# A long convolution on one core: the order of products, sums and inverses in the middle phase

## The chip, the cores and the metric

The kernel runs on one core of a Trainium2 chip. The time is the device time of one execution in microseconds; before the change it is the median of three runs. The engines are named as in the profile: PE (matrix products, with its weight loads as PEld), DVE (vector), ACT (scalar), POOL (GpSimd) and SP (which here only starts DMAs). Each works through its own instructions in order and waits for others by semaphores.

## The reference, cut to what matters

```python
def _attn_ref(x, v, pos_emb, w1, w2):            # x, v: 4 x 12800 x 128
    h_mlp = np.maximum(pos_emb @ w1, 0.0) @ w2
    h_filt = h_mlp * np.exp(-0.01 * pos)[:, None]
    u = x * v
    Uf = np.fft.rfft(u, n=2 * S, axis=1)
    Hf = np.fft.rfft(h_filt, n=2 * S, axis=0)
    y = np.fft.irfft(Uf * Hf[None], n=2 * S, axis=1)[:, :S]
    return x * y

def _moe_ref(x, w_val, conv_w, w_out):           # x is the result above
    gate_pre = sum(conv_w[k] * xp[:, k:k + S] for k in range(5))
    return (sigmoid(gate_pre) * (x @ w_val)) @ w_out
```

A causal convolution over 12800 positions is done by Fourier transforms, for 4 batches and 128 channels, and followed by a gated projection. All of it is in float32.

## The kernel before, in words

The sequence is split in J = 2 halves, and each half of 6400 positions into N1 = 100 times N2 = 64. The transform is done in two steps, with three phases one after the other, each with its own buffers:

1. The first transform step over the signal (and the filter's own transform). It writes its result `a_u` to DRAM.
2. The **middle phase**, which alone is changed: for each of the 100 outer frequencies the second transform step, the product with the filter's spectrum, and the first step of the way back. It reads `a_u`, works on two frequencies at a time (a pair; NP = 50 pairs) and writes `c_y` to DRAM.
3. The last step of the inverse transform, then gate and projection.

In the middle phase one pair p is made of the following.

- `load_pair(p)`: SP starts the load of the pair's part of `a_u` (1 MB), and every fourth pair that of a table of weights. Loads run two pairs ahead (`AHEAD`), in six buffers named `ld`.
- `filter_pair(p)`: four short products on PE, and three ACT instructions that put the filter's spectrum into `h_sb`.
- `spectrum(..., j, c)`: one product z of signal half j, real or imaginary part c, into one PSUM buffer `z_ps`. There are four such products a pair, called z00, z01, z10 and z11 here (half, part). The four `z_ps` buffers are used in turn, and the filter takes one as well: five a pair from four buffers.
- `times(...)`: DVE multiplies a z (from PSUM) with the filter (SBUF). From half 0: `va` (z00) and `vb` (z01), each of four blocks of 512 columns; from half 1: `vc` (z10) and `vd` (z11), each of two blocks.
- The sums. Output half 0 needs va[0:2] + vb[0:2]. Output half 1 needs va[2:4] + vb[2:4] + vc + vd. That is four additions of 128 x 1024, three on POOL and one on DVE.
- `inverse(p, j, v)`: four products on PE into `c_ps` (two buffers), and an ACT copy into `c_sb`. When both halves of a pair are in `c_sb`, ACT starts two DMAs to `c_y`.

A matmul of z or of the filter reads all 128 rows and writes 64 columns of the array; one of the inverse reads 64 rows and writes 128 columns. Two such matmuls stand side by side on the array as a pair. Each product in float32 is two instructions per matmul in the profile, so a z shows as x4, a filter and an inverse as x8.

The order on each engine in this phase is the order in which the code is written (`tc.manual_schedule()`); nothing is moved by a scheduler. The loop runs over periods: in one period the products of pair p, the sums of pair p and the inverses of pair p - 1 are issued. Before the change PE's order in a period is z10 and z11 of p, inverse 0 of p - 1, filter and z00 of p + 1, inverse 1 of p - 1, z01 of p + 1. On DVE it is va, vb, the add of p - 1 (L432), vc, vd. On POOL: va[0:2] + vb[0:2] (L441), vc + vd (L442), va[2:4] + vb[2:4] (L443).

Phases 1 and 3 are not touched; in the changed file their line numbers are five smaller behind the change.

Of the kernel before, what the change touches and what calls it, by code (L numbers as in the profile page):

```python
# [118 lines left out]
def tile_longconv_gate(  # L119
# [205 lines left out]
    with tc.tile_pool(name="p2", bufs=1) as p2, tc.tile_pool(name="ps2", bufs=1, space=PSUM) as ps2:  # L325
# [10 lines left out]
        def filter_pair(p):  # L336

            h_ps = bank().rearrange("p (c e) -> p c e", c=2)
            for c in range(2):
                for h in range(2):  # L340
                    nc.tensor.matmul(
                        out=h_ps[half[h], c], lhsT=ag[:, 2 * p + h].rearrange("p j e -> p (j e)")[:, half[c]],
                        rhs=w2bd.rearrange("p j d -> p (j d)"), start=True, stop=True)
            h_sb = p2.tile([128, 2, J, 2, D], F32, name="h_sb2", bufs=3)
            src = h_ps.rearrange("p c (j d) -> p c j d", j=J)
            nc.scalar.copy(out=h_sb[:, 0].rearrange("p j c d -> p c j d"), in_=src)
            nc.scalar.activation(h_sb[:, 1, :, 0], src[:, 1], AF.Copy, scale=-1.0)
            nc.scalar.copy(out=h_sb[:, 1, :, 1], in_=src[:, 0])
            return h_sb

        def spectrum(a2, wk, j, c):
            z = bank()
            for h in range(2):
                nc.tensor.matmul(out=z[half[h]], lhsT=wk[:, h, half[c]], rhs=a2[:, h, j], start=True, stop=True)  # L354
            return z
# [21 lines left out]
        def inverse(p, j, vt):  # L377
            wk = loaded[p][1]
            c_ps = ps2.tile([128, 2, BD], F32, name="c_ps", bufs=2)
            for c in range(2):  # L380
                for h in range(2):
                    nc.tensor.matmul(  # L382
                        out=c_ps[:, h], lhsT=wk[half[h], 2 + c], rhs=vt[half[h], c].rearrange("p b d -> p (b d)"),
                        start=(c == 0), stop=(c == 1))
            if j == 0:
                c_sb = p2.tile([128, 2, J, B, D], F32, name="c_sb", bufs=2)
                outs[p] = c_sb
            c_sb = outs[p]
            nc.scalar.copy(out=c_sb[:, :, j].rearrange("p h b d -> p h (b d)"), in_=c_ps)  # L389
            if j == J - 1:  # L390
                for h in range(2):
                    nc.scalar.dma_start(
                        out=c_y[:, 2 * p + h].rearrange("j p b d -> p j (b d)"),
                        in_=c_sb[:, h].rearrange("p j b d -> p j (b d)"))

        weights, loaded, outs = [], {}, {}
        filt_p, z0, v_p = {}, {}, {}
        AHEAD = 2

        def start_pair(p):  # L400
            filt_p[p] = filter_pair(p).rearrange("p s j c d -> p s (j c) d")

        def first(p):
            z0[p, 0] = spectrum(*loaded[p], 0, 0)

        def second(p):
            z0[p, 1] = spectrum(*loaded[p], 0, 1)

        with tc.manual_schedule():
            for p in range(-1, NP + 1):
                now, nxt, old = 0 <= p < NP, p + 1 < NP, 0 <= p - 1
                for q in range(AHEAD + 1) if p < 0 else (p + AHEAD,):
                    if q < NP and q not in loaded:
                        loaded[q] = load_pair(q)
                if now:
                    h = filt_p.pop(p)
                    z10 = spectrum(*loaded[p], 1, 0)
                    z11 = spectrum(*loaded[p], 1, 1)  # L420
                    va = p2.tile([128, 2 * J, B, D], F32, name="va", bufs=3)
                    vb = p2.tile([128, 2 * J, B, D], F32, name="vb", bufs=2)
                    times(va, z0.pop((p, 0)), h[:, 0], 2 * J)
                    times(vb, z0.pop((p, 1)), h[:, 1], 2 * J)
                if old:
                    oa, oc = v_p.pop(p - 1)
                    inverse(p - 1, 0, oa)
                if nxt:
                    start_pair(p + 1)
                    first(p + 1)  # L430
                if old:
                    nc.vector.tensor_tensor(oc, oc, oa[:, 2:4], op=ALU.add)  # L432
                    inverse(p - 1, 1, oc)
                if nxt:
                    second(p + 1)
                if now:
                    vc = p2.tile([128, 2, B, D], F32, name="vc", bufs=3)
                    vd = p2.tile([128, 2, B, D], F32, name="vd", bufs=2)
                    times(vc, z10, h[:, 0, 0:2], 2)
                    times(vd, z11, h[:, 1, 0:2], 2)  # L440
                    nc.gpsimd.tensor_tensor(va[:, 0:2], va[:, 0:2], vb[:, 0:2], op=ALU.add)  # L441
                    nc.gpsimd.tensor_tensor(vc, vc, vd, op=ALU.add)  # L442
                    nc.gpsimd.tensor_tensor(va[:, 2:4], va[:, 2:4], vb[:, 2:4], op=ALU.add)  # L443
                    v_p[p] = va, vc

    ag_pool.__exit__(None, None, None)

# [234 lines left out]
```

## Time and profile before

| | |
|---|---|
| runs | 1241.81, 1249.56, 1248.66 us; median 1248.66 |
| profiled execution | 1245.33 us, span from first to last instruction 1243.6 us |
| mean granted TensorE clock | 0.955 |
| busy | PE 1091.5 us (88%), DVE 981.3 (79%), POOL 707.4 (57%), ACT 621.4 (50%) |
| middle phase | first POOL addition at 379.1 us, last copy of `c_sb` at 809.6 us |
| DMA | 332.96 MB, 268 GB/s on average |

A span's rows give start, duration, engine, line of the kernel, operation, the tiles written and read, and in brackets how long the engine was idle before it and what ended that. `x8` means that eight instructions were put together in a row. `DVE L432` is the DVE addition of the sums, `POOL L441` to `L443` are POOL's. The ends of matmuls are modelled, so PE is read by starts. Where several events are waited for, the row names the one that came last by the profile, and that name can be of another engine than the real cause.

### The profile page before, as it was taken

How to read it: one execution, taken by the hardware profiler on the slowest of the kernel's cores; microseconds unless marked ns; L12 is line 12 of the kernel's file. 1: busy time of each engine (PE TensorE's matmuls, PEld its weight loads, DVE VectorE, ACT ScalarE, POOL GpSimd, SP SyncE). 2: the span in 40 equal slices, each digit the busy share in tenths (PEclk: the TensorE clock that was granted, in tenths of full speed). 3: DMA queues.
4: the chain of work that ended last, by engine and by line, in shares of the span. 5: the costliest groups of instructions: out<-in, count | busy, mean ns of one | idle time of the engine just before them, and what ended most of it. 6: DMA issues, size and time to landing. Idle time of an engine off the chain costs nothing. (4 is left out here: it accounts for less than half of the span.)

```text
span 1243.6 us, 15440 instructions
## 1 busy us (share of the span) xinstructions
PE 1091.5 (88%) x5244; PEld 483.2 (39%) x5244; DVE 981.3 (79%) x1133; ACT 621.4 (50%) x1000; POOL 707.4 (57%) x282
## 2 busy tenths in 40 slices
PE   2578999768759999999999999878999999999886
PEld 1344666433323333333333333333444444444442
DVE  6576444567719999999999999706999899999897
ACT  1234755667642343343333333316667666766763
POOL 0000000000005899999999999806898888898890
PEclk9789999888878999999999999969999999999999
DMA  9999999999976777778778776388899999999932
GB/s 215 276 307 338 337 318 320 293 298 344 304 257 254 262 275 269 271 279 298 277 275 297 275 279 241 135 233 221 244 280 284 270 263 267 288 271 263 294 133 105
DMA packets 78151, 332.96 MB, mean 268 GB/s; under 512 B 8622, under 2 KB 9818, under 8 KB 57338
## 3 DMA queue, kind: packets, MB, share of 16 engines
q1 hardware_dynamic: 36928, 202.00, 55.0%
q10 hardware_dynamic: 41146, 129.98, 28.7%
q8 instruction: 43, 0.70, 0.2%
q14 instruction: 34, 0.28, 0.1%
HBM read 200.87 MB, written 131.07 MB: 267 GB/s over the span
## 5 line engine op out<-in xcount | busy, mean ns | idle before, releaser
L441 POOL TENSOR_TENSOR va<-va,vb 128x1024 f32<-128x1024 f32 x50 | 156.9, 3138 | 397.8 <-DVE vb L359 397.8
L542 POOL TENSOR_TENSOR ext<-yr,xr 128x400 f32<-128x400 f32 x120 | 301.1, 2511 | 55.7 <-DVE yr L540 35.8
L557 DVE SCALAR_TENSOR_TENSOR gt<-ext,cw,gt 128x1600 f32<-128x1600 f32 x128 | 241.3, 1885 | 1.1 <-ACT gt L554 1.1
L389 ACT COPY c_sb<-c_ps 128x1024 f32<-128x1024 f32 x100 | 101.3, 1013 | 274.1 <-PE c_ps L382 269.7
L354 PE MATMUL z_ps<-ld 128*64 128x512 f32 x800 | 196.7, 611 | 12.2 <-DMA ld<-a_u 12.2
L286 ACT COPY st<-fp 100x1024 f32<-100x1024 f32 x128 | 130.0, 1030 | 123.7 <-PE fp L285 46.0
L258 DVE TENSOR_TENSOR xv<-xv 114x1024 f32<-114x1024 f32 x64 | 78.4, 1224 | 116.7 <-DMA xv<-in_xv_dram 115.8
L515 PE MATMUL sd<-ld,inv 100*64 100x512 f32 x512 | 132.1, 622 | 9.8 <-DMA ld<-c_y 9.8
L576 PE MATMUL o_ps<-gd,wout 128*128 128x400 f32 x256 | 112.6, 522 | 26.3 <-ACT o_sb L584 12.0
L359 DVE TENSOR_TENSOR vb<-z_ps,h_sb 128x2048 f32<-128x2048 f32 x50 | 114.5, 2291 | 25.1 <-ACT c_sb L389 24.7
L359 DVE TENSOR_TENSOR va<-z_ps,h_sb 128x2048 f32<-128x2048 f32 x50 | 114.0, 2279 | 24.7 <-DMA ld<-a_u 24.7
L442 POOL TENSOR_TENSOR vc<-vc,vd 128x1024 f32<-128x1024 f32 x50 | 118.2, 2364 | 15.4 <-DVE vd L359 10.3
L443 POOL TENSOR_TENSOR va<-va,vb 128x1024 f32<-128x1024 f32 x50 | 118.5, 2370 | 0.0
L522 ACT COPY sd_sb<-sd 128x512 f32<-128x512 f32 x128 | 76.5, 598 | 75.3 <-PE sd L515 64.2
L382 PE MATMUL c_ps<-vc,ld 64*128 64x512 f32 x400 | 101.7, 627 | 9.2 <-DVE vc L432 8.8
L566 PE MATMUL v_ps<-ext,wval 128*128 128x400 f32 x256 | 107.6, 502 | 0.0
L354 PEld LDWEIGHTS z_ps<-ld 128*64 128x64 f32 x800 | 55.3, 139 | 118.6 <-issue 91.7
L382 PE MATMUL c_ps<-va,ld 64*128 64x512 f32 x400 | 99.4, 615 | 0.1
L285 PE MATMUL fp<-us,fsd 64*100 64x512 f32 (+1 forms) x256 | 76.9, 680 | 23.1 <-ACT st L286 21.7
L539 DVE TENSOR_TENSOR yr<-tp,dif 128x204 f32<-128x204 f32 x128 | 45.8, 358 | 61.7 <-ACT dif L531 61.6
L529 PEld LDWEIGHTS tp<-ident,sd_sb 128*128 128x128 f32 x512 | 59.8, 143 | 78.1 <-PE sd L515 49.5
L529 PE MATMUL tp<-ident,sd_sb 128*128 128x128 f32 x512 | 81.6, 285 | 3.6 <-DVE yr L540 3.6
(74 smaller groups left out, 1623.7 us busy)
## 6 DMA issues: line engine op xcount, KB each, us to landing
c_y<-c_sb ACTq DMA_DIRECT2D x100, 512.0 KB
ld<-a_u SPq DMA_DIRECT2D x49, 1024.0 KB
xv<-in_xv_dram SPq DMA_DIRECT2D x64, 768.0 KB
a_u<-st ACTq DMA_DIRECT2D x64, 768.0 KB
ld<-c_y SPq DMA_DIRECT2D x64, 768.0 KB
xr<-in_xt_dram SPq DMA_DIRECT2D x32, 800.0 KB
out_dram<-o_sb ACTq DMA_DIRECT2D x32, 800.0 KB
ld<-in_tab_w_dram SPq DMA_DIRECT2D x12, 1024.0 KB
```

What stands on the lines that cost most here:

```text
L286: nc.scalar.copy(out=st[:, c], in_=fp.rearrange("k j e -> k (j e)"))
L354: nc.tensor.matmul(out=z[half[h]], lhsT=wk[:, h, half[c]], rhs=a2[:, h, j], start=True, stop=True)
L359: nc.vector.tensor_tensor(out, z.rearrange("p (b d) -> p b d", d=D).unsqueeze(1).to_broadcast([128, n, B, D]), h_sb.unsqueeze(2).to_broadc ...
L382: nc.tensor.matmul(out=c_ps[:, h], lhsT=wk[half[h], 2 + c], rhs=vt[half[h], c].rearrange("p b d -> p (b d)"), start=(c == 0), stop=(c == 1))
L441: nc.gpsimd.tensor_tensor(va[:, 0:2], va[:, 0:2], vb[:, 0:2], op=ALU.add)
L442: nc.gpsimd.tensor_tensor(vc, vc, vd, op=ALU.add)
L443: nc.gpsimd.tensor_tensor(va[:, 2:4], va[:, 2:4], vb[:, 2:4], op=ALU.add)
L515: nc.tensor.matmul(out=sd[c * N2:(c + 1) * N2], lhsT=inv[:, c], rhs=ct[c][:, r * B * D:(r + 1) * B * D], start=True, stop=True)
L529: nc.tensor.transpose(out=tp[:, b], in_=t[:, b], identity=ident)
L542: nc.gpsimd.tensor_tensor(e[:, r0 + r], yr, xr, op=ALU.mult)
L557: nc.vector.scalar_tensor_tensor(gt, rows(t, k), cw[:, k:k + 1], gt, op0=ALU.mult, op1=ALU.add)
L576: nc.tensor.matmul(out=o_ps, lhsT=wout, rhs=gd, start=True, stop=True)
```

## The change

The work is the same, in another order. In a period PE now runs z00 and z01 of p, the filter of p + 1, z10 and z11 of p in one run, then inverse 1 and inverse 0 of p - 1 in one run. The sum for output half 1 is built up in another order: POOL adds vb[2:4] to va[2:4], then adds vc to that, then does va[0:2] + vb[0:2]; DVE adds the result of the second to vd, one period later, between its va and its vb. `vc` has two buffers in place of three, `vd` three in place of two. `c_sb` is begun by half 1 and sent off after half 0.

```diff
-            if j == 0:
+            if j == J - 1:
                 c_sb = p2.tile([128, 2, J, B, D], F32, name="c_sb", bufs=2)
                 outs[p] = c_sb
...
-            if j == J - 1:
+            if j == 0:
                 for h in range(2):
                     nc.scalar.dma_start(
...
+        def add(eng, out, a, b):
+            eng.tensor_tensor(out, a, b, op=ALU.add)
...
         with tc.manual_schedule():
-            for p in range(-1, NP + 1):
-                now, nxt, old = 0 <= p < NP, p + 1 < NP, 0 <= p - 1
-                for q in range(AHEAD + 1) if p < 0 else (p + AHEAD,):
-                    if q < NP and q not in loaded:
-                        loaded[q] = load_pair(q)
-                if now:
-                    h = filt_p.pop(p)
-                    z10 = spectrum(*loaded[p], 1, 0)
-                    z11 = spectrum(*loaded[p], 1, 1)
+            for q in range(AHEAD):
+                loaded[q] = load_pair(q)
+            h_next, old = filt_of(0), None
+            for p in range(NP + 1):
+                if p + AHEAD < NP:
+                    loaded[p + AHEAD] = load_pair(p + AHEAD)
+                if p < NP:
+                    h = h_next
+                    z = {}
+                    for c in range(2):
+                        z[0, c] = spectrum(*loaded[p], 0, c)
                     va = p2.tile([128, 2 * J, B, D], F32, name="va", bufs=3)
                     vb = p2.tile([128, 2 * J, B, D], F32, name="vb", bufs=2)
-                    times(va, z0.pop((p, 0)), h[:, 0], 2 * J)
-                    times(vb, z0.pop((p, 1)), h[:, 1], 2 * J)
-                if old:
-                    oa, oc = v_p.pop(p - 1)
-                    inverse(p - 1, 0, oa)
-                if nxt:
-                    start_pair(p + 1)
-                    first(p + 1)
-                if old:
-                    nc.vector.tensor_tensor(oc, oc, oa[:, 2:4], op=ALU.add)
-                    inverse(p - 1, 1, oc)
-                if nxt:
-                    second(p + 1)
-                if now:
-                    vc = p2.tile([128, 2, B, D], F32, name="vc", bufs=3)
-                    vd = p2.tile([128, 2, B, D], F32, name="vd", bufs=2)
-                    times(vc, z10, h[:, 0, 0:2], 2)
-                    times(vd, z11, h[:, 1, 0:2], 2)
-                    nc.gpsimd.tensor_tensor(va[:, 0:2], va[:, 0:2], vb[:, 0:2], op=ALU.add)
-                    nc.gpsimd.tensor_tensor(vc, vc, vd, op=ALU.add)
-                    nc.gpsimd.tensor_tensor(va[:, 2:4], va[:, 2:4], vb[:, 2:4], op=ALU.add)
-                    v_p[p] = va, vc
+                    times(va, z[0, 0], h[:, 0], 2 * J)
+                if old is not None:
+                    add(nc.vector, old[1], old[1], old[0][:, 2:4])
+                if p < NP:
+                    times(vb, z[0, 1], h[:, 1], 2 * J)
+                    if p + 1 < NP:
+                        h_next = filt_of(p + 1)
+                    for c in range(2):
+                        z[1, c] = spectrum(*loaded[p], 1, c)
+                    vc = p2.tile([128, 2, B, D], F32, name="vc", bufs=2)
+                    vd = p2.tile([128, 2, B, D], F32, name="vd", bufs=3)
+                    times(vc, z[1, 0], h[:, 0, 0:2], 2)
+                    times(vd, z[1, 1], h[:, 1, 0:2], 2)
+                if old is not None:
+                    inverse(p - 1, 1, old[1])
+                    inverse(p - 1, 0, old[0])
+                if p < NP:
+                    add(nc.gpsimd, va[:, 2:4], va[:, 2:4], vb[:, 2:4])
+                    add(nc.gpsimd, va[:, 2:4], va[:, 2:4], vc)
+                    add(nc.gpsimd, va[:, 0:2], va[:, 0:2], vb[:, 0:2])
+                    old = va, vd
```

On POOL this is what stands in the queue for one pair in the middle of the phase, with what each instruction waits for; the numbers behind the names tell the buffers' generations apart. First before, from one pair's L441 to the next pair's:

```order
L441 TENSOR_TENSOR va_2594<-va_2594,vb_2595 128x1024 [waits DVE_49,Pool_49]
L442 TENSOR_TENSOR vc_2629<-vc_2629,vd_2630 128x1024 [waits DVE_49]
L443 TENSOR_TENSOR va_2594<-va_2594,vb_2595 128x1024
L441 TENSOR_TENSOR va_2644<-va_2644,vb_2645 128x1024 [waits DVE_49,Pool_49]
L442 TENSOR_TENSOR vc_2679<-vc_2679,vd_2680 128x1024 [waits DVE_49]
```

After the change all three come from the helper `add` (L403); the first is va[2:4] + vb[2:4], the second va[2:4] + vc, the third va[0:2] + vb[0:2]:

```order
L403 TENSOR_TENSOR va_2588<-va_2588,vb_2589 128x1024 [waits DVE_49]
L403 TENSOR_TENSOR va_2588<-va_2588,vc_2608 128x1024 [waits DVE_49,Pool_49]
L403 TENSOR_TENSOR va_2588<-va_2588,vb_2589 128x1024
L403 TENSOR_TENSOR va_2638<-va_2638,vb_2639 128x1024 [waits DVE_49]
L403 TENSOR_TENSOR va_2638<-va_2638,vc_2658 128x1024 [waits DVE_49,Pool_49]
```

The second addition waits for POOL's own first one, and the third waits for nothing of its own. On DVE, at about the same place, before:

```order
L359 TENSOR_TENSOR va_2594<-z_ps_2564,h_sb2_2560 128x2048 [waits DVE_49,PE_49,Activation_49]
L359 TENSOR_TENSOR vb_2595<-z_ps_2576,h_sb2_2560 128x2048 [waits PE_49,Activation_49]
L432 TENSOR_TENSOR vc_2579<-vc_2579,va_2544 128x1024 [waits DVE_49,Pool_49]
L359 TENSOR_TENSOR vc_2629<-z_ps_2588,h_sb2_2560 128x1024 [waits PE_49]
L359 TENSOR_TENSOR vd_2630<-z_ps_2591,h_sb2_2560 128x1024 [waits PE_49]
```

And after:

```order
L359 TENSOR_TENSOR va_2588<-z_ps_2582,h_sb2_2548 128x2048 [waits PE_49,Activation_49]
L403 TENSOR_TENSOR vd_2559<-vd_2559,va_2538 128x1024 [waits DVE_49,Pool_49]
L359 TENSOR_TENSOR vb_2589<-z_ps_2585,h_sb2_2548 128x2048 [waits PE_49,Activation_49]
L359 TENSOR_TENSOR vc_2608<-z_ps_2602,h_sb2_2548 128x1024 [waits PE_49]
L359 TENSOR_TENSOR vd_2609<-z_ps_2605,h_sb2_2548 128x1024 [waits PE_49]
```

The addition has moved from behind vb to between va and vb, and what it reads from POOL (va of the pair before) is now written by POOL's second addition of that pair instead of its third. On PE, before, from an inverse 0 to the next inverse 1 (a product that is several instructions of the profile is one or two rows here):

```order
L382 MATMUL c_ps_2548<-va_2494,ld_2378 128x512 [waits Pool_49]
L382 MATMUL c_ps_2548<-va_2494,ld_2378 128x512 x3
L341 MATMUL z_ps_2555<-w2bd_70,ag_90 64x256 [waits DVE_49]
L341 MATMUL z_ps_2555<-w2bd_70,ag_90 64x256 x3
L354 MATMUL z_ps_2564<-ld_2486,ld_2484 64x512 [waits DMAHW5_49,DMAHW4_49,DVE_49]
L354 MATMUL z_ps_2564<-ld_2486,ld_2484 64x512
L382 MATMUL c_ps_2568<-vc_2529,ld_2378 128x512 [waits DVE_49,Activation_49]
L382 MATMUL c_ps_2568<-vc_2529,ld_2378 128x512 x3
```

And after, from the filter, the third of the five products of a run, to the end of the inverses:

```order
L341 MATMUL z_ps_2543<-w2bd_70,ag_90 64x256 [waits DVE_49]
L341 MATMUL z_ps_2543<-w2bd_70,ag_90 64x256 x3
L354 MATMUL z_ps_2552<-ld_2428,ld_2378 64x512 [waits DVE_49]
L354 MATMUL z_ps_2552<-ld_2428,ld_2378 64x512
L354 MATMUL z_ps_2555<-ld_2428,ld_2378 64x512 [waits DVE_49]
L354 MATMUL z_ps_2555<-ld_2428,ld_2378 64x512
L382 MATMUL c_ps_2562<-vd_2509,ld_2378 128x512 [waits DVE_49,Activation_49]
L382 MATMUL c_ps_2562<-vd_2509,ld_2378 128x512 x3
L382 MATMUL c_ps_2569<-va_2488,ld_2378 128x512 [waits Activation_49,Pool_49]
L382 MATMUL c_ps_2569<-va_2488,ld_2378 128x512 x3
```

The two inverses (c_ps) now stand one behind the other, and z11 (z_ps_2555) waits for DVE to have read the buffer that it takes over.

More of the change, by code (lines that the diff above doesn't have):

```diff
@@ L396, in tile_longconv_gate, with filt_of @@
         weights, loaded, outs = [], {}, {}
-        filt_p, z0, v_p = {}, {}, {}
         AHEAD = 2
[L400 to L407, printed above, removed]
-        with tc.manual_schedule():
-            for p in range(-1, NP + 1):
-                now, nxt, old = 0 <= p < NP, p + 1 < NP, 0 <= p - 1
-                for q in range(AHEAD + 1) if p < 0 else (p + AHEAD,):
-                    if q < NP and q not in loaded:
-                        loaded[q] = load_pair(q)
-                if now:
-                    h = filt_p.pop(p)
-                    z10 = spectrum(*loaded[p], 1, 0)
-                    z11 = spectrum(*loaded[p], 1, 1)
+        def filt_of(p):
+            return filter_pair(p).rearrange("p s j c d -> p s (j c) d")
```

## The prediction

> **What bounds the kernel now.** I read the table of stages first, for the middle phase, which alone is changed.
>
> ```profile
> core 0: us, PE busy (x) PEld busy (x) DVE busy (x) ACT busy (x) POOL busy (x), PEclk, DMA share, GB/s
> 386.00:397.00 11.00, 8.25 (x30) 2.42 (x28) 10.54 (x6) 2.13 (x4) 7.57 (x5) 0.84 0.40 153
> ...
> 407.50:418.00 10.50, 8.57 (x32) 2.69 (x30) 10.05 (x6) 2.41 (x5) 6.76 (x4) 0.84 0.50 185
> ...
> 450.00:500.00 50.00, 50.00 (x240) 17.38 (x238) 46.72 (x31) 18.98 (x30) 46.89 (x19) 1.00 0.82 291
> ```
>
> From 450 to 500 us PE is never idle at full clock; DVE and POOL are at 94%. Everything is close to its limit, so what an instruction waits for matters more than its length. Near 390 and 410 us it is otherwise: DVE is full and PE idle for 2 to 3 us in 11. Next the timeline, one period of the steady part (start, duration, engine):
>
> ```profile
> 560.16 1.99 PE L382 MATMUL c_ps<-va,ld 64*128 64x512 f32 x8
> 560.84 1.22 DVE L432 TENSOR_TENSOR vc<-vc,va 128x1024 f32<-128x1024 f32 x1
> 561.06 3.22 POOL L441 TENSOR_TENSOR va<-va,vb 128x1024 f32<-128x1024 f32 x1 [0.40 <-DVE vb L359]
> 561.97 1.22 DVE L359 TENSOR_TENSOR vc<-z_ps,h_sb 128x1024 f32<-128x1024 f32 x1
> 562.08 1.08 PE L341 MATMUL z_ps<-w2bd,ag 128*64 128x256 f32 x8
> 562.99 1.03 PE L354 MATMUL z_ps<-ld 128*64 128x512 f32 x4
> 563.95 1.99 PE L382 MATMUL c_ps<-vc,ld 64*128 64x512 f32 x8
> 564.23 2.28 DVE L359 TENSOR_TENSOR va<-z_ps,h_sb 128x2048 f32<-128x2048 f32 x1
> 565.87 2.79 PE L354 MATMUL z_ps<-ld 128*64 128x512 f32 x12
> 566.35 0.14 PEld L354 LDWEIGHTS z_ps<-ld 128*64 128x64 f32 x2 [0.28 <-issue]
> 566.72 2.37 POOL L443 TENSOR_TENSOR va<-va,vb 128x1024 f32<-128x1024 f32 x1
> 567.06 2.29 DVE L359 TENSOR_TENSOR vb<-z_ps,h_sb 128x2048 f32<-128x2048 f32 x1 [0.55 <-ACT c_sb L389]
> 567.63 0.14 PEld L354 LDWEIGHTS z_ps<-ld 128*64 128x64 f32 x2 [0.29 <-issue]
> 568.59 1.99 PE L382 MATMUL c_ps<-va,ld 64*128 64x512 f32 x8
> ```
>
> The period is 568.59 - 560.16 = 8.43 us, and PE fills it. Look at the two engines at 560.84: the DVE add starts first, POOL's add 0.22 later, and POOL's takes 3.22 where the other POOL add here takes 2.37. Both read two SBUF operands. Which of them starts first is the whole question, and the first periods of the phase show the other case:
>
> ```profile
> 379.10 2.37 POOL L441 TENSOR_TENSOR va<-va,vb 128x1024 f32<-128x1024 f32 x1 [378.66 <-DVE vb L359]
> ...
> 383.76 2.36 POOL L443 TENSOR_TENSOR va<-va,vb 128x1024 f32<-128x1024 f32 x1
> ...
> 386.08 2.34 POOL L441 TENSOR_TENSOR va<-va,vb 128x1024 f32<-128x1024 f32 x1
> 386.15 3.35 DVE L432 TENSOR_TENSOR vc<-vc,va 128x1024 f32<-128x1024 f32 x1 [0.48 <-POOL va L443]
> ...
> 389.43 1.21 DVE L359 TENSOR_TENSOR vc<-z_ps,h_sb 128x1024 f32<-128x1024 f32 x1
> 389.56 2.41 PE L382 MATMUL c_ps<-vc,ld 64*128 64x512 f32 x8 [2.75 <-DVE vc L432]
> ...
> 391.90 4.02 PE L354 MATMUL z_ps<-ld 128*64 128x512 f32 x12
> ...
> 396.48 2.35 POOL L441 TENSOR_TENSOR va<-va,vb 128x1024 f32<-128x1024 f32 x1
> 396.56 3.36 DVE L432 TENSOR_TENSOR vc<-vc,va 128x1024 f32<-128x1024 f32 x1 [0.30 <-POOL va L443]
> ...
> 406.91 2.36 POOL L441 TENSOR_TENSOR va<-va,vb 128x1024 f32<-128x1024 f32 x1
> 406.99 3.37 DVE L432 TENSOR_TENSOR vc<-vc,va 128x1024 f32<-128x1024 f32 x1 [0.40 <-POOL va L443]
> ...
> 410.50 2.87 PE L382 MATMUL c_ps<-vc,ld 64*128 64x512 f32 x8 [1.93 <-DVE vc L432]
> 411.41 1.21 DVE L359 TENSOR_TENSOR vd<-z_ps,h_sb 128x1024 f32<-128x1024 f32 x1
> ...
> 412.70 2.36 POOL L442 TENSOR_TENSOR vc<-vc,vd 128x1024 f32<-128x1024 f32 x1 [3.43 <-DVE vd L359]
> ...
> 415.26 2.29 DVE L359 TENSOR_TENSOR vb<-z_ps,h_sb 128x2048 f32<-128x2048 f32 x1 [0.45 <-PE z_ps L354]
> ...
> 417.47 1.22 DVE L432 TENSOR_TENSOR vc<-vc,va 128x1024 f32<-128x1024 f32 x1
> 417.70 3.23 POOL L441 TENSOR_TENSOR va<-va,vb 128x1024 f32<-128x1024 f32 x1 [0.32 <-DVE vb L359]
> ```
>
> Three times the DVE add waited for L443's result. It then started 0.07 to 0.08 us after POOL's next add, and took 3.35 to 3.37 us, not 1.22: it ended 1.07 to 1.09 us after POOL did. The add that comes second is held until the first is through. Those periods are 10.41 and 10.43 us long. At 417.47 a late vb delayed POOL's add, DVE came first, and POOL's add paid 0.86 us out of its own slack instead. From then on the period was 8.43.
>
> [...]
>
> **The change, part by part.**
>
> *PE.* The weight loads from 566.35 to 567.63 are three steps of a pair of matmuls each, 1.28 us, so 0.43 a pair. Three products are six pairs, 2.58 us, and their run takes 568.59 - 565.87 = 2.72: 0.14 for entering and leaving it. An inverse is four pairs, 1.72, and takes 562.08 - 560.16 = 1.92: 0.20. Each period has two runs of each kind, after the change one. PE's work falls by 0.34 to 8.09 us a period. That is worth 17 us only if PE stays the bound.
>
> *POOL and DVE.* Still three POOL adds and one DVE add, of the same shapes; no instruction goes. But the DVE add now reads va[2:4] after both vb and vc were added to it, and POOL's remaining add (va[0:2]) stands right behind that one, with no wait of its own. This is L443, L441 and L432 of the first periods again: DVE waits for a POOL result, and POOL's next add is always on its way before DVE hears of it. In the steady part of before the competing add, L441, needs vb, which stands directly ahead of the DVE add on DVE: DVE goes on at once, POOL hears of it later (417.47 against 417.70), and L443 is through by then (566.72 + 2.37 = 569.09, vb's end 569.35). After the change the competing add needs a vb that was done two POOL adds earlier, and the result that DVE waits for is the one just ahead of it. So I take the held length in every period.
>
> The loop that closes then: held add, times into vb, first POOL add, second POOL add, and the held add again. Step by step:
> - held add to the next DVE start: 389.43 - 386.15 = 3.28
> - vb: 2.29
> - from DVE's end to a POOL add that waits for it alone: 412.70 - (411.41 + 1.21) = 0.08
> - va[2:4] += vb: 2.36
> - POOL waiting for its own result, which before does not show. Low end 0.03: POOL's end to DVE's start, 386.15 - (383.76 + 2.36). High end 0.15: 417.70 - (415.26 + 2.29), DVE to a POOL add with two waits. I take 0.08, a single wait's row; the ends move the sum by -2.5 and +3.4 us over 49 periods
> - va[2:4] += vc until va[0:2] += vb starts: 386.08 - 383.76 = 2.32
> - from there to the DVE add: 0.08
>
> The sum is **10.49 us a period**, against 8.43.
>
> *What lies beside it.* PE has to bring inverse 1, inverse 0 and the next z between two held adds, and then va must be written: 0.14 (add's end at 406.99 + 3.37 to PE's start at 410.50), two inverses 3.84, z to its product on DVE 1.19 (565.87 to 567.06), va up to the following start 2.21 (2.28 less the 0.07 by which DVE starts its next instruction early, 389.43 against 386.15 + 3.35), an add without a hold 1.22: 8.60 of 10.49. So 1.89 us are spare, and the saved 0.34 lies in PE's idle time, worth nothing. If that cover went, the loop would be longer by what exceeds 1.89. Two waits are new. z11 takes z00's buffer of the four and so waits for DVE's va; behind it on PE stand the inverses, which need the add, and that is later anyway. POOL's second add waits for the first; behind it on POOL stands va[0:2], for which inverse 0 waits and which holds DVE, and both are in the loop above. ACT copies both c_sb halves one after the other, 2 x 1.01 in a period where it is busy 38%. The c_y DMAs go out once a period as before, and SP's loads wait for PE reads that are further apart; at 0.82 DMA share with 8.43 us there is more room at 10.49. vc's two buffers are written again two periods on, vd's three after three; POOL and inverse 1 have read them within one and two, so that delays nothing. Phases 1 and 3 keep their order.
>
> *The sum.* The end of before, first all 50 DVE adds (durations in ns, least, median, most; first and last start), then the last copy:
>
> ```profile
> L432 DVE TENSOR_TENSOR vc<-vc,va x50: 1215/1216/3368, 386.2 to 805.2; 128x1024 f32<-128x1024 f32 x50
> ```
>
> ```profile
> 809.60 1.01 ACT L389 COPY c_sb<-c_ps 128x1024 f32<-128x1024 f32 x1 [6.10 <-PE c_ps L382]
> ```
>
> The last of 50 adds starts at 805.2, the last c_sb copy at 809.60, 3.2 us behind the add's end. After the change POOL's first add starts at 379.10 as now, since vb of pair 0 is made as before. Its third add ends 2.36 + 0.08 + 2.32 + 2.35 = 7.11 later; 49 periods are 514.0; so POOL's last add ends at 900.2, the held add at 901.3, and the last copy comes 3.2 + 1.8 behind, since two inverses stand at the end: 906.3. That is 96.7 us later. Of this 46 x 2.06 = 95 is the hold; the three periods that were held already gain nothing. The profiled execution took 1245.33 us (span 1243.6), so 1342.0. The median of the runs, 1248.66, lies 3.3 above it; between 1342 and 1345.3 I say **1343**.
>
> **The rivals.**
>
> *The add is not held.* If DVE's add gets in ahead of POOL's third, DVE goes on after 1.13 (560.84 to 561.97), and the loop is 1.13 + 2.29 + 0.08 + 2.36 + 0.08 + 2.37 + 0.03 = 8.34, a little under today's 8.43. With the first three periods no longer held (3 x 2.1) and 46 x 0.09 that is 10 us less: 1236 to 1239, no slower, within 1%. It decides if DVE hears of the second add before POOL starts the third, so at the 0.07 us by which POOL led. Against it: three of three such meetings went to POOL. 0.05.
>
> *PE stays the bound and the merged runs pay.* Then 8.09 a period and the three periods free: 24 us less, 1222. It needs the two dependent POOL adds and vb inside 8.09, 0.25 less than the unheld loop has by its rows. 0.02.
>
> *The clock.* PE will idle about 2.4 us in 10.5. In the two stretches of the first view the granted clock is 0.84, and the run at 391.90 takes 4.02 instead of 2.79, that at 389.56 2.41 instead of 1.99: 1.65 together, still inside the 1.89. Two such slow spells in one period would cost 3.3, 1.4 over the spare time; in every third of 49 periods that is 23 us: 1366. 0.07.
> [...]
>
> **How the numbers follow.** Held add, PE within its spare time: 0.86, at 1343, from 1339 to 1348 by the bounds of POOL's own wait and the 3.3 us between profile and median. The range goes up to the clock's rival, and a few us down for what I have rounded: 1333 to 1366, which leaves out the two cases without a hold, 0.07, and worse clocks. A change of under 1% can't be told from none in this kernel. Slower by over 1%: 0.93 (held 0.86, clock 0.07); within 1%: 0.05; faster: 0.02.
>
> **What would show it.** In the changed profile the DVE add should take 3.3 to 3.4 us in nearly all of its 49 ordinary cases, start about 0.08 us after POOL's third add has started, and name POOL as what it waited for; POOL's third add should take 2.36, none 3.2. The period should be 10.4 to 10.6, with PE idle over 2 us in it ahead of the inverse and its runs without the two extra switches. I am wrong if DVE adds take 1.22 while POOL's take 3.2 (the order is not what I read from three rows), if the period is past 10.8 (PE's clock, or a longer wait of POOL on itself), or if phases 1 and 3 move by more than the spread of 1241.81 to 1249.56.

## The result, and the profile after

| | before | after |
|---|---|---|
| median of the runs made side by side | 1244.18 us (6 runs, 1241.26 to 1249.56) | 1346.26 us (6 runs, 1342.49 to 1354.44) |
| profiled execution, span | 1245.33 us, 1243.6 us | 1346.61 us, 1344.8 us |
| mean granted TensorE clock | 0.955 | 0.935 |
| last `c_sb` copy of the middle phase | 809.60 us | 905.92 us |

The ratio is 1.0804, with a 95% interval of 1.0767 to 1.0841: the change makes the kernel slower by 8%. Of the 101.2 us by which the span grew, 96.3 lie ahead of the last copy of the middle phase.

The table of stages for the middle phase after the change (length, busy time and number of instructions of each engine, granted clock, DMA share, GB/s):

```profile
core 0: us, PE busy (x) PEld busy (x) DVE busy (x) ACT busy (x) POOL busy (x), PEclk, DMA share, GB/s
...
450.00:500.00 50.00, 41.08 (x200) 16.04 (x200) 47.43 (x25) 15.81 (x25) 34.01 (x15) 1.00 0.63 225
550.00:600.00 50.00, 43.88 (x200) 17.18 (x196) 43.72 (x25) 15.62 (x25) 32.87 (x15) 0.93 0.68 236
```

Compare the first row with that of before: PE fell from 50.00 to 41.08 of 50 us, POOL from 46.89 to 34.01, and the DMA share from 0.82 to 0.63. DVE alone is as full as it was (47.43 against 46.72), though it ran 25 instructions and not 31. An engine that is as busy with fewer instructions has longer ones. All instructions of the helper `add`, grouped (durations in ns, least, median, most; first and last start), show which:

```profile
L403 POOL TENSOR_TENSOR va<-va,vb x100: 2330/2360/2383, 378.6 to 897.2; 128x1024 f32<-128x1024 f32 x100
...
L403 POOL TENSOR_TENSOR va<-va,vc x50: 2338/2370/2379, 381.0 to 894.9; 128x1024 f32<-128x1024 f32 x50
L403 DVE TENSOR_TENSOR vd<-vd,va x50: 1215/3297/3347, 383.4 to 897.3; 128x1024 f32<-128x1024 f32 x50
```

The median DVE add went from 1216 to 3297 ns. POOL's additions are all between 2330 and 2383: none of them takes 3.2 us any more. The timeline of one steady period:

```profile
598.92 2.37 POOL L403 TENSOR_TENSOR va<-va,vb 128x1024 f32<-128x1024 f32 x1 [3.36 <-DVE vb L359]
...
601.37 2.37 POOL L403 TENSOR_TENSOR va<-va,vc 128x1024 f32<-128x1024 f32 x1
...
601.62 2.29 DVE L359 TENSOR_TENSOR va<-z_ps,h_sb 128x2048 f32<-128x2048 f32 x1 [0.52 <-ACT c_sb L389]
...
603.71 2.34 POOL L403 TENSOR_TENSOR va<-va,vb 128x1024 f32<-128x1024 f32 x1
...
603.83 3.30 DVE L403 TENSOR_TENSOR vd<-vd,va 128x1024 f32<-128x1024 f32 x1
...
607.05 2.28 DVE L359 TENSOR_TENSOR vb<-z_ps,h_sb 128x2048 f32<-128x2048 f32 x1
...
607.28 1.99 PE L382 MATMUL c_ps<-vd,ld 64*128 64x512 f32 x8 [2.23 <-DVE vd L403]
...
609.41 2.38 POOL L403 TENSOR_TENSOR va<-va,vb 128x1024 f32<-128x1024 f32 x1 [3.37 <-DVE vb L359]
...
610.91 1.94 PE L354 MATMUL z_ps<-ld 128*64 128x512 f32 x8
...
614.32 3.31 DVE L403 TENSOR_TENSOR vd<-vd,va 128x1024 f32<-128x1024 f32 x1
```

POOL's third addition starts at 603.71, the DVE add 0.12 us behind it, and the add ends at 607.13, 1.08 us after POOL. Then vb follows, POOL waits 3.37 us for vb, and its next chain of three begins. The add itself shows no wait: POOL's second addition is through at 603.74, and DVE's own va, at 603.91, is through last. The period is 614.32 - 603.83 = 10.49 us. PE idles 2.23 us ahead of the inverse in it, and the two inverses, one behind the other, take 610.91 - 607.28 = 3.63.

### The profile page after: what moved, and what is told of

Same layout as the page of the kernel before. It is cut to its first block, busy times and chain, and to the rows that moved or that the text cites. A ratio compares the mean times of both kernels' runs of the same rounds, so it can differ in the third digit from the quotient of the medians.

```text
span 1344.8 us, 15454 instructions
## 1 busy us (share of the span) xinstructions
PE 1105.9 (82%) x5244; PEld 505.5 (38%) x5244; DVE 1053.7 (78%) x1133; ACT 622.7 (46%) x1000; POOL 668.2 (50%) x282
## 5 line engine op out<-in xcount | busy, mean ns | idle before, releaser
L403 POOL TENSOR_TENSOR va<-va,vb 128x1024 f32<-128x1024 f32 x100 | 235.9, 2359 | 543.1 <-DVE vb L359 543.1
L389 ACT COPY c_sb<-c_ps 128x1024 f32<-128x1024 f32 x100 | 101.2, 1012 | 289.0 <-PE c_ps L382 289.0
L382 PE MATMUL c_ps<-vd,ld 64*128 64x512 f32 x400 | 119.3, 718 | 92.8 <-DVE vd L403 92.7
L403 DVE TENSOR_TENSOR vd<-vd,va 128x1024 f32<-128x1024 f32 x50 | 139.4, 2788 | 3.1 <-POOL va L403 3.1
L403 POOL TENSOR_TENSOR va<-va,vc 128x1024 f32<-128x1024 f32 x50 | 118.3, 2366 | 3.9
L382 PEld LDWEIGHTS c_ps<-vd,ld 64*128 64x128 f32 x400 | 43.5, 209 | 160.9 <-issue 155.3
L382 PE MATMUL c_ps<-va,ld 64*128 64x512 f32 x400 | 103.8, 632 | 0.0
L354 PEld LDWEIGHTS z_ps<-ld 128*64 128x64 f32 x800 | 49.7, 136 | 126.0 <-issue 48.4
```

The lines of the kernel that those rows point to most:

```text
L382: nc.tensor.matmul(out=c_ps[:, h], lhsT=wk[half[h], 2 + c], rhs=vt[half[h], c].rearrange("p b d -> p (b d)"), start=(c == 0), stop=(c == 1))
L403: eng.tensor_tensor(out, a, b, op=ALU.add)
```

## The experiments

The theory: the new order makes the DVE add start behind POOL's third addition in every period; both read two operands from SBUF, the add is held until POOL's addition is through (3.30 us, where most adds of before take 1.22), and this closes a loop of 10.49 us. One rival says that the longer chain of dependent additions is what costs; another that DVE and POOL merely slow each other whenever they meet. Periods below are from the starts of like instructions in the profiled execution; those read from two rows lie within 0.02 us of the mean over the steady part.

### One operand of the add from PSUM

```diff
-                    add(nc.vector, old[1], old[1], old[0][:, 2:4])
+                    if p < NP:
+                        zb = z[0, 1].rearrange("p (b d) -> p b d", d=D).unsqueeze(1).to_broadcast([128, 2, B, D])
+                        nc.vector.tensor_tensor(old[1], zb, old[0][:, 2:4], op=ALU.add)
+                    else:
+                        add(nc.vector, old[1], old[1], old[0][:, 2:4])
```

> The changed kernel, with one operand of the DVE add taken from PSUM (the product z01 of the running pair) in place of vd, so that it reads one SBUF operand; its wait for POOL's second addition, its place and its length stay. (The summand vd is left out of the result.) Theory of the hold (a DVE instruction with two SBUF operands that starts after a POOL addition waits until that is through): the add takes 1.22 us beside POOL's third addition, the period falls from 10.49 to the longer of the loop through POOL, 8.34, and that through PE, 8.41; the time is 1346 - 49 x 2.05, about 1246. Rival, the chain (two dependent POOL additions and a wait set the period, and the long add only fills the waiting time): 10.49 stays, 1346. Rival, sharing (both engines slow down while they overlap, whoever starts): the add is somewhere between, about 2.2, the period about 9.5, 1297.

Measured: 1247.4 us (10 runs), 0.999 of before (0.9954 to 1.0025). In the timeline of this kernel:

```profile
598.42 2.36 POOL L403 TENSOR_TENSOR va<-va,vb 128x1024 f32<-128x1024 f32 x1
598.49 1.23 DVE L423 TENSOR_TENSOR vd<-z_ps,va 128x1024 f32<-128x1024 f32 x1
...
599.86 1.99 PE L382 MATMUL c_ps<-vd,ld 64*128 64x512 f32 x8 [0.16 <-DVE vd L423]
...
606.91 1.23 DVE L423 TENSOR_TENSOR vd<-z_ps,va 128x1024 f32<-128x1024 f32 x1
```

The meeting is the same, 0.07 us behind POOL's third addition, but the add takes 1.23 us and the period is 8.42. The order of POOL's chain and the wait for its result are unchanged, so the chain alone doesn't cost the 2 us, and with one of its operands in PSUM the add isn't held here at all. What bounds now is the loop that the prediction put beside the held one: add 1.23, start of PE 0.14, two inverses 3.63, z to DVE 1.19, va 2.21, together 8.40. The inverses wait 0.16 for the add in each period, so even without the hold the merged runs of PE bring nothing in this order.

### POOL's third addition halved

```diff
-                    add(nc.gpsimd, va[:, 0:2], va[:, 0:2], vb[:, 0:2])
+                    add(nc.gpsimd, va[:, 0:1], va[:, 0:1], vb[:, 0:1])
```

> The changed kernel with POOL's third addition half as wide (512 columns in place of 1024; block 1 of va stays without its summand). Theory of the hold: that addition takes about 1.19 us, the DVE add ends 1.08 us after it and so takes about 2.15, the period falls by 1.17 to 9.32, the time by 57 to about 1289. Rival, the chain: the third addition is not in it, so 10.49 and 1346 stay. Rival, PE's clock: 10.49 stays.

Measured: 1295.07 us (4 runs), 1.0412 of before (1.0328 to 1.0496). Its timeline:

```profile
601.92 1.28 POOL L403 TENSOR_TENSOR va<-va,vb 128x512 f32<-128x512 f32 x1
602.05 2.23 DVE L403 TENSOR_TENSOR vd<-vd,va 128x1024 f32<-128x1024 f32 x1
...
611.47 2.23 DVE L403 TENSOR_TENSOR vd<-vd,va 128x1024 f32<-128x1024 f32 x1
```

With a POOL addition shorter by 1.08 us the DVE add is shorter by 1.07 (2.23 against 3.30) and ends 1.08 us after POOL again. The period is 9.41: what POOL's addition is shorter by, the loop is shorter by too. The expectation was off only in the length of the halved addition, 1.19 for 1.28.

### POOL's third addition put first

```diff
+                    add(nc.gpsimd, va[:, 0:2], va[:, 0:2], vb[:, 0:2])
                     add(nc.gpsimd, va[:, 2:4], va[:, 2:4], vb[:, 2:4])
                     add(nc.gpsimd, va[:, 2:4], va[:, 2:4], vc)
-                    add(nc.gpsimd, va[:, 0:2], va[:, 0:2], vb[:, 0:2])
```

> The changed kernel with POOL's additions in another order: va[0:2] + vb[0:2] first, then the two that the DVE add needs, so that POOL has nothing under way when that add starts. Theory of the hold: every DVE add takes 1.22, but the moved addition now stands in the loop itself: 1.13 + 2.29 + 0.08 + 2.33 + 2.36 + 0.08 + 2.37 + 0.03 = 10.67 a period, about 1355, no gain. Had the long add been the only cost, with no loop behind it, the period would fall to about 8.4 and the time to 1246.

Measured: 1358.39 us (4 runs), 1.0911 of before (1.0827 to 1.0996). Its timeline:

```profile
603.71 2.35 POOL L403 TENSOR_TENSOR va<-va,vc 128x1024 f32<-128x1024 f32 x1
606.10 1.23 DVE L403 TENSOR_TENSOR vd<-vd,va 128x1024 f32<-128x1024 f32 x1 [2.19 <-POOL va L403]
...
616.75 1.23 DVE L403 TENSOR_TENSOR vd<-vd,va 128x1024 f32<-128x1024 f32 x1 [2.16 <-POOL va L403]
```

Nothing holds the add, it takes 1.23, and nothing is gained, since three POOL additions now stand between vb and the add where there were two. The period is 10.67 (10.65 between these two rows). An add that waits and one that is held cost the loop nearly the same, about the length of the third addition. A short DVE add is therefore no proof of a good order.

### The order of before with the add one place later

```diff
+                if now:
+                    vc = p2.tile([128, 2, B, D], F32, name="vc", bufs=3)
+                    vd = p2.tile([128, 2, B, D], F32, name="vd", bufs=2)
+                    times(vc, z10, h[:, 0, 0:2], 2)
                 if old:
                     nc.vector.tensor_tensor(oc, oc, oa[:, 2:4], op=ALU.add)
                     inverse(p - 1, 1, oc)
...
                 if now:
-                    vc = p2.tile([128, 2, B, D], F32, name="vc", bufs=3)
-                    vd = p2.tile([128, 2, B, D], F32, name="vd", bufs=2)
-                    times(vc, z10, h[:, 0, 0:2], 2)
```

> The kernel before with one thing moved: its DVE add (and the inverse behind it) stands behind the times that makes vc, not ahead of it, so that POOL's first addition has started about 0.9 us before it. No dependence is added. Theory of the hold: the add is held until POOL's is through and takes about 2.5 us, POOL's additions all take 2.36, and the loop of POOL's addition, the held add, vd and the two other POOL additions is 2.36 + 1.08 + 1.13 + 0.08 + 2.33 + 2.33 = 9.3 a period; with 46 periods of 0.87 more, 1244 + 40 = 1284. Rival, sharing: the order of start does not matter, POOL's first addition still takes 3.2 and the DVE add 1.22, the period stays 8.43, 1244.

Measured: 1285.63 us (4 runs), 1.0318 of before (1.0233 to 1.0403). Its timeline, without anything of the change but the lost start:

```profile
603.42 2.37 POOL L442 TENSOR_TENSOR va<-va,vb 128x1024 f32<-128x1024 f32 x1
604.16 2.71 DVE L436 TENSOR_TENSOR vc<-vc,va 128x1024 f32<-128x1024 f32 x1
...
613.47 2.72 DVE L436 TENSOR_TENSOR vc<-vc,va 128x1024 f32<-128x1024 f32 x1
```

The same dependences as before, but POOL is first by 0.74 us: the add ends 1.08 us after POOL (606.87 against 605.79), the POOL additions no longer show 3.22 (all 150 take 2.34 to 2.38), and the period is 9.31. It matters who starts first, so the two don't merely slow each other, and the remainder of POOL's addition is the price. Nor is it that both engines touch one buffer of va: here POOL works on the va of pair p and the add reads that of pair p - 1, and with the PSUM operand the add reads the va that POOL's third addition works on and isn't held.

### The third addition as a pure write

```diff
-                    add(nc.gpsimd, va[:, 0:2], va[:, 0:2], vb[:, 0:2])
+                    nc.gpsimd.memset(va[:, 0:2], 0.0)
```

> The changed kernel with POOL's third addition replaced by a POOL memset of the same 128 x 1024 block, which writes SBUF and reads none (that block of va is lost). Theory of the hold in its narrow form (only a POOL instruction that reads SBUF holds the DVE add): the add takes 1.22, the period is 8.42 as with the PSUM operand, the time about 1246. Wider form (any POOL instruction on SBUF holds it): the add ends about 1.1 us after the memset; for a memset of 1.1 us that is an add of 2.1 and a period of 9.3.

Measured in a single run: 1254.52 us. A place in its timeline:

```profile
606.10 0.96 POOL L438 MEMSET va<- 128x1024 f32 x1
606.26 1.22 DVE L403 TENSOR_TENSOR vd<-vd,va 128x1024 f32<-128x1024 f32 x1
```

The add reads two SBUF operands as in the changed kernel and runs beside a POOL instruction that started first, for 0.80 us of its length, and still takes 1.22: this POOL instruction, which only writes, doesn't hold it. With the first experiment this narrows the hold from both sides: the add of the changed kernel that took 3.30 had both of its operands in SBUF, and the POOL instruction that came first read SBUF too; with one operand in PSUM it took 1.23, and beside the memset 1.22. The time of this single run is 8 us above what was expected, though all 50 adds take 1.22 or 1.23 and the period is 8.40. Most of that lies ahead of the middle phase, which the edit doesn't touch: POOL's first addition starts at 391.42 us, and at 383.10 in the kernel with the PSUM operand. Some more is the hand-over to phase 3 spoken of further down, which takes 7.3 us here.

### The merged runs with the meeting taken away

Here the wait itself is moved out of the loop. DVE adds vd to vc by itself, one pair behind, directly after vb, where before's order let it start first (560.84 against POOL's 561.06); POOL adds that sum in another period; the inverses run two pairs behind. `vc` has three buffers again and `vd` two.

```diff
-                if old is not None:
-                    add(nc.vector, old[1], old[1], old[0][:, 2:4])
...
+                if p - 1 in vs:
+                    add(nc.vector, vs[p - 1][1], vs[p - 1][1], vs[p - 1][2])
...
-                if old is not None:
-                    inverse(p - 1, 1, old[1])
-                    inverse(p - 1, 0, old[0])
+                if p - 2 in vs:
+                    oa = vs.pop(p - 2)[0]
+                    inverse(p - 2, 1, oa[:, 2:4])
+                    inverse(p - 2, 0, oa[:, 0:2])
                 if p < NP:
-                    add(nc.gpsimd, va[:, 2:4], va[:, 2:4], vb[:, 2:4])
-                    add(nc.gpsimd, va[:, 2:4], va[:, 2:4], vc)
                     add(nc.gpsimd, va[:, 0:2], va[:, 0:2], vb[:, 0:2])
+                    add(nc.gpsimd, va[:, 2:4], va[:, 2:4], vb[:, 2:4])
+                    vs[p] = va, vc, vd
+                if p - 1 in vs:
+                    oa, oc, _ = vs[p - 1]
+                    add(nc.gpsimd, oa[:, 2:4], oa[:, 2:4], oc)
...
```

> The merged PE runs of the change, with the sums arranged so that DVE waits for no POOL result: DVE adds vd to vc of the pair before right behind vb (it starts ahead of POOL's first addition, which needs that vb), POOL adds va[0:2] + vb[0:2], va[2:4] + vb[2:4] and, for the pair before, the DVE sum to va[2:4]; both inverses are those of pair p - 2. Theory of the hold: DVE adds take 1.22 and POOL's first additions 3.2, as before the change; POOL needs 3.2 + 2.33 + 2.33, about 7.9, DVE 7.81, PE 8.09, and the loop of va (2.29), z11 (1.0), two inverses (3.63) and z00 up to va (1.20) 8.13. The period is 8.1 to 8.2, no period at the start is held, and the time is 46 x 0.30 + 3 x 2.2, about 20 us, below the kernel before: 1224, ratio 0.984. Rival, merging the runs is worth nothing by itself: the period stays at 8.43 and the time near 1238 (no held periods at the start).

Measured: 1264.14 us (12 runs), 1.0116 of before (1.0074 to 1.0158). A miss. Its waits from 450 to 800 us (total, times, longest), and a place in its timeline:

```profile
PEld c_ps L382 <- POOL va L403: 52.2, 40, 1.8
```

```profile
606.50 2.36 POOL L403 TENSOR_TENSOR va<-va,vc 128x1024 f32<-128x1024 f32 x1
608.92 3.70 PE L382 MATMUL c_ps<-va,ld 64*128 64x512 f32 x16 [0.90 <-POOL va L403]
```

The hold is gone, but I had put the addition that inverse 1 needs last on POOL and inverse 1 first on PE, so PE waits for POOL in every period, 52.2 / 40 = 1.3 us on average by its weight loads. The next three kernels separate that from the rest.

The same sums with PE in the order of before (inverses apart, each of its products where it stood); its edit against the kernel before, for DVE and PE alone (`last` is 0 <= p - 1 < NP, `old` now 0 <= p - 2):

```diff
+                if last:
+                    add(nc.vector, v_p[p - 1][1], v_p[p - 1][1], v_p[p - 1][2])
                 if old:
-                    oa, oc = v_p.pop(p - 1)
-                    inverse(p - 1, 0, oa)
+                    oa = v_p.pop(p - 2)[0]
+                    inverse(p - 2, 0, oa[:, 0:2])
                 if nxt:
                     start_pair(p + 1)
                     first(p + 1)
                 if old:
-                    nc.vector.tensor_tensor(oc, oc, oa[:, 2:4], op=ALU.add)
-                    inverse(p - 1, 1, oc)
+                    inverse(p - 2, 1, oa[:, 2:4])
...
```

> The same sums and inverses two pairs behind, but PE's order of before, with an inverse between the products twice a period. Theory: PE's work is 8.43 us again and sets the period; the three held periods at the start go (3 x 2.0): about 6 us below before, 1238, ratio 0.995. What merging the PE runs is worth is the difference to the run with merged runs, 0.30 x 49, about 15 us. If the late inverses and not the merged runs made the gain, both runs would have the same time.

Measured: 1243.71 us (12 runs), 0.9948 of before (0.9914 to 0.9982).

```profile
599.08 2.29 DVE L359 TENSOR_TENSOR va<-z_ps,h_sb 128x2048 f32<-128x2048 f32 x1 [0.54 <-PE c_ps L382]
...
607.51 2.29 DVE L359 TENSOR_TENSOR va<-z_ps,h_sb 128x2048 f32<-128x2048 f32 x1 [0.55 <-PE c_ps L382]
```

The period is 8.43 as in before's steady part. What is gained, about 5 us, is the held periods at the start of the phase: POOL's first addition starts at 379.11 as before, the fourth DVE add at 409.52 and not at 417.47. Of these 8 us some are given back at the end, where the inverses run one period more.

The merged runs again, with POOL's two other additions exchanged (edit against `late_inverses`):

```diff
...
                     add(nc.gpsimd, va[:, 0:2], va[:, 0:2], vb[:, 0:2])
-                    add(nc.gpsimd, va[:, 2:4], va[:, 2:4], vb[:, 2:4])
-                    vs[p] = va, vc, vd
                 if p - 1 in vs:
                     oa, oc, _ = vs[p - 1]
                     add(nc.gpsimd, oa[:, 2:4], oa[:, 2:4], oc)
+                if p < NP:
+                    add(nc.gpsimd, va[:, 2:4], va[:, 2:4], vb[:, 2:4])
+                    vs[p] = va, vc, vd
```

> The merged runs with late inverses, with POOL's last two additions exchanged: the addition that inverse 1 waits for comes second, 2.3 us earlier. In the run before this one PE waited 0.8 to 1.8 us a period for it (8.21 and 9.19 us in turn). Theory: that wait goes, the period is that of va, z11, two inverses and z00, 8.13, close to PE's own 8.09; the time 46 x 0.30 + 6 = 20 below the kernel before, ratio 0.984. Rival, merged runs gain nothing even with all sums ready: 8.43, ratio 0.995 as with the unmerged order.

Measured: 1232.51 us (6 runs), 0.988 of before (0.982 to 0.994), with the lowest median of all the kernels here. Its stage, and one period of the timeline:

```profile
450.00:500.00 50.00, 50.00 (x248) 18.49 (x246) 48.03 (x31) 19.07 (x31) 48.33 (x19) 1.00 0.84 299
```

```profile
600.23 3.70 PE L382 MATMUL c_ps<-va,ld 64*128 64x512 f32 x16
...
601.28 1.22 DVE L403 TENSOR_TENSOR vc<-vc,vd 128x1024 f32<-128x1024 f32 x1
601.44 3.28 POOL L403 TENSOR_TENSOR va<-va,vb 128x1024 f32<-128x1024 f32 x1 [0.28 <-DVE vb L359]
...
603.86 1.94 PE L354 MATMUL z_ps<-ld 128*64 128x512 f32 x8
...
605.09 2.29 DVE L359 TENSOR_TENSOR va<-z_ps,h_sb 128x2048 f32<-128x2048 f32 x1 [0.33 <-ACT c_sb L389]
...
607.43 0.20 PEld L354 LDWEIGHTS z_ps<-ld 128*64 128x64 f32 x4 [0.79 <-DVE va L359]
...
608.44 1.99 PE L382 MATMUL c_ps<-va,ld 64*128 64x512 f32 x8
```

DVE starts first again (601.28 against 601.44), POOL pays 0.92 us out of its own time, and the period is 608.44 - 600.23 = 8.21. I had expected 8.13, and the loop that I expected closes in these rows. z11 takes the buffer of z00, which is free when va is done (605.09 + 2.29 = 607.38), and its weight load follows at 607.43. From z00 to va it is 1.23 us, va takes 2.29, from its end to the inverses it is 1.06, and from the inverses to the next z00 3.63 (600.23 to 603.86): 8.21, where I had 1.20, 2.29, 1.0 and 3.63. The 0.08 lies in the two hand-overs between PE and DVE. That a fifth buffer of `z_ps` would save more is not shown: no such kernel was run.

And in place of that exchange, inverse 0 ahead of inverse 1 (edit against `late_inverses`; `c_sb` is begun by half 0 and sent off after half 1 again):

```diff
...
-                    inverse(p - 2, 1, oa[:, 2:4])
                     inverse(p - 2, 0, oa[:, 0:2])
+                    inverse(p - 2, 1, oa[:, 2:4])
```

> The merged runs with late inverses, with inverse 0 ahead of inverse 1 instead; POOL's order is kept. Inverse 0 needs an addition of a whole period earlier, and inverse 1, now 1.7 us later, needs one that ends about 0.6 us before. Theory: the same 8.13 a period, ratio 0.984, with less to spare; if POOL comes late in some periods, up to 8.3, ratio 0.99. Rival, merged runs gain nothing: 8.43, ratio 0.995.

Measured: 1237.88 us (12 runs), 0.9917 of before (0.9877 to 0.9958), with a profiled span of 1230.7 us against 1230.4 for the exchanged one; the two can't be told apart. Its DVE adds from 450 to 780 us start 8.21 or 8.22 us apart, as those of the exchanged one do. Two independent ways of taking away the wait of PE for POOL lead to the same 8.21, so that wait was the miss of `late_inverses` but for the last 0.08 us a period. Merging the runs is then worth 8.43 - 8.21 = 0.22 us a period of the 0.34 by which PE's work falls: with POOL's additions exchanged the last copy comes at 797.23 us where the unmerged kernel has it at 805.15, though its first POOL addition starts 2.8 us later (381.89 against 379.11).

## Why the prediction was right, point by point

**The loop.** Said 10.49 us a period; the starts of the DVE adds give (897.29 - 383.44) / 49 = 10.487. Its least certain term, POOL's wait for its own result (0.03 to 0.15, taken as 0.08), is 601.37 - (598.92 + 2.37) = 0.08. Held add to the next DVE start is 607.05 - 603.83 = 3.22 in place of 3.28, and the add starts 0.12 behind POOL's in place of 0.08; the two nearly cancel. The last copy was to come at 906.3 and came at 905.92. That it is so close is in part luck: POOL's first addition started 0.5 us earlier than before (378.60), and from the end of the last add to the last copy it took 5.3 us in place of 5.0.

**The hold in every period.** The mechanism held, the count did not: I said 3.3 to 3.4 us "in nearly all of its 49 ordinary cases". It is 35 of the 50; 14 take 1.59 to 1.68, and the second takes 1.22, not held at all. One of those fourteen, in the timeline after:

```profile
876.42 3.30 DVE L403 TENSOR_TENSOR vd<-vd,va 128x1024 f32<-128x1024 f32 x1
...
879.87 3.60 PE L382 MATMUL c_ps<-vd,ld 64*128 64x512 f32 x8 [2.23 <-DVE vd L403]
...
885.12 3.65 PE L354 MATMUL z_ps<-ld 128*64 128x512 f32 x16
...
886.31 2.29 DVE L359 TENSOR_TENSOR va<-z_ps,h_sb 128x2048 f32<-128x2048 f32 x1 [2.13 <-ACT c_sb L389]
...
886.76 2.36 POOL L403 TENSOR_TENSOR va<-va,vb 128x1024 f32<-128x1024 f32 x1
...
888.52 1.68 DVE L403 TENSOR_TENSOR vd<-vd,va 128x1024 f32<-128x1024 f32 x1
...
897.29 3.34 DVE L403 TENSOR_TENSOR vd<-vd,va 128x1024 f32<-128x1024 f32 x1 [2.62 <-POOL va L403]
```

Here PE was late (inverse 1 at 879.87 took 3.60 us where 1.99 is usual), DVE waited 2.13 us for its z00, and POOL was nearly through (889.12) when the add started. It is held for the rest alone and again ends 1.08 us after POOL, at 890.20. From start to start the two periods are 12.10 and 8.77 us; from end to end of the adds (879.72, 890.20, 900.63) they are 10.48 and 10.43. POOL's chain kept its pace while PE was late, so the short adds are no gain and the late PE is no loss. What the prediction left out is that a late va comes out of the held time of the add: it had the price of a slow spell and the spare time that covers it, but not what the adds would show.

**Who releases the add.** The sign "name POOL as what it waited for" did not come: only the first and the last of the 50 adds do. In the others DVE's own va is through last. From the add's end the way through PE and va takes 0.15 + 3.63 + 1.20 + 2.21 = 7.19 us to the next add (607.13 to 614.32), that through POOL about 7.13 (7.06 to its third addition at 614.19, and 0.07 more, by the first add). The prediction had the add start right behind POOL's second addition; that it came second all the same isn't luck, for the add can't start before that result, and POOL's third addition waits for nothing. And the period goes by POOL even so: the add ends 1.08 us after POOL at whatever time it starts beside POOL's third addition, as at 888.52.

**The clock.** That rival had 23 us for slow spells, and they came: PEclk is 0.93 from 550 to 600. One spell in a period fits into the spare time, as the prediction had it. From inverse 1 to z00 it is 885.12 - 879.87 = 5.25 us where 607.28 to 610.91 is 3.63, so 1.62 more, and by the measured terms 10.49 - 8.40 = 2.09 are spare. Fourteen periods lose 1.6 to 1.7 us in this way, and it costs nothing. More than the spare time was lost once: before the second add these steps took 6.00 us (386.84 to 392.84), 2.37 more, and that add ends 10.67 us after the first, 0.2 late. So the rival's way of costing time was right, and it came once and not in every third period.

**PE's saved work** was put at nothing. The two inverses in a row take 3.63 us where I had 3.84, so the merging does save what it should, and PE idles 2.23 us in the same period. Right.

**The rival without a hold** was priced at 8.34 a period, 1236 to 1239 us. The kernel with the PSUM operand is that rival: 8.42 and 1247.4. I priced only the loop through POOL there and forgot my own loop through PE, 8.60 by the prediction's terms and 8.40 by the measured ones, which is then the longer one.

**The end.** 4.9 us of the growth lie behind the last copy and were not in the sum, which carried phase 3 over unchanged. The hand-over in the timeline, before:

```profile
810.64 0.89 ACTq L392 DMA_DIRECT2D c_y<-c_sb  x2
...
814.98 0.82 SPq L470 DMA_DIRECT2D xr<-in_xt_dram  x2
...
838.99 1.94 PE L515 MATMUL sd<-ld,inv 100*64 100x512 f32 x8
```

And after:

```profile
906.96 0.89 ACTq L392 DMA_DIRECT2D c_y<-c_sb  x2
...
913.15 0.82 SPq L465 DMA_DIRECT2D xr<-in_xt_dram  x2
...
937.96 1.94 PE L510 MATMUL sd<-ld,inv 100*64 100x512 f32 x8
```

From the last DMA of `c_y` to the first load of phase 3 it is 6.19 us and not 4.34; at the fourth run of phase 3's first products (the last row of each) the delay against the last copy is 2.65 us (32.04 against 29.39), and the other 2.2 us come later in that phase. From the last copy to this load the other kernels take 5.4 to 7.3 us, before 5.4 and after 7.2; no run here takes the cause apart, and it stays open.

## What to carry to other kernels

When an addition is moved, ask which instruction of the other engine stands next in its queue at that moment and who will start first: the DVE add needs a POOL result behind which POOL's next addition starts at once, so it met that addition in all but one of 50 periods and came second, mostly by 0.1 us, which turned 1.22 us into 3.30 in the loop that sets the period. Close the loop on paper, engine by engine, before counting what another engine saves; PE's 0.34 us a period was worth nothing until the sums no longer waited for one another, and 0.22 then. And the cure was to take the wait out of the period (sums and inverses one pair later), for merely putting POOL's third addition first changed a hold into a wait of about the same cost (10.67 us a period against 10.49).

## What the runs showed of the hardware

In these runs the hold is narrower than two engines at work on SBUF at once, and a little shorter than the whole add. The held add ended 1.08 us after POOL in the changed kernel, with POOL's addition halved, and with the add moved in the order of before: 0.14 us less than the 1.22 that an add takes which isn't held. A POOL memset of 0.96 us did not hold it (1.22), nor was it held with one operand in PSUM (1.23).

The granted clock fell to 0.84 from 875 to 886 us, next to PE idle times of 2.23 us only:

```profile
875.00:886.00 11.00, 8.77 (x36) 3.36 (x34) 9.18 (x5) 2.93 (x5) 7.56 (x4) 0.84 0.26 96
```

Even the weight loads idle for no more than 3.1 us at a time from 450 to 897 us. The gap alone doesn't make a spell: the same 2.23 us stand ahead of the inverse at 607.28, which takes the usual 1.99, at a granted clock of 1.00 from 605 to 610.9. The spells come in a rhythm. The slow runs of inverse 1 start at 523.41, 544.38, 565.34 and 586.30 us, every second period, and the same four come again 146.8 us later, from 670.17, and once more from 816.97. What sets that rhythm was not found.
